# The first layer's first weights decoded from a later attention step on, and a pair's pooled values summed six steps later

## The chip, the core and the metric

The program runs on one core of one Trainium2 chip. The metric is the device time of one execution in microseconds (us), from launch to end. The kernel before took 979.33 us (median of three runs, 978.94 to 981.45). The core has five instruction streams that count here: PE (TensorE, matmuls, with its weight loads listed as PEld), DVE (VectorE), ACT (ScalarE), POOL (GpSimd) and SP (SyncE), which only issues DMAs. Each engine takes its list in order, and a semaphore holds it at an instruction whose inputs or buffers aren't ready.

## The reference

Three stages follow each other. First an attention with two parts, for 4 batches, 8 heads, 576 positions and 64 features a head: one on values averaged over groups of four positions, spread out again, and a local one in which a position sees the three neighbours on either side. Their sum, laid out as 2304 tokens of 512 features, goes through two layers of the same shape, the first with SiLU, the second with ELU.

```python
q_d, k_d, v_d = (z.reshape(B, H, S // 4, 4, D).mean(axis=3) for z in (q, k, v))
out_up = np.repeat(sm_attn(q_d, k_d, v_d), 4, axis=2)
mask = np.abs(pos[:, None] - pos[None, :]) < 4
attn = softmax(np.where(mask, q @ k.T / 8, -1e9))
x = (out_up + attn @ v).transpose(0, 2, 1, 3).reshape(B * S, H * D)
h = x @ w_in            # 2304x512 by 512x2048
x = (h * sigmoid(h)) @ w_out
h = x @ w_in2
out = np.where(h > 0, h, np.exp(np.minimum(h, 0)) - 1) @ w_out2
```

q, k, v and the weights arrive as they are drawn; the weights of both layers are 64-bit floats.

## The kernel before

**Attention.** Two heads are one pair, so there are 16 pairs, numbered 0 to 15, four a batch. `attention(i)` (L282) is a generator with 18 yields, so 19 steps: one call of `step()` (L681) advances one live pair to its next yield, so that several pairs are interleaved in the lists of all engines. Its parts, in order: transposition of q and k on PE (L297) with copies by ACT (L305, L307); the sums over four positions (L310, DVE); local scores (L319, PE, tile `psl`) with mask (L326) and maximum (L333) on DVE and the subtraction on POOL (L334); **the pooled values**, two additions of four rows of v into `vt` (L341) and one into `vd` (L342), all on POOL; the loads of the next pair (`load_pair`) and of this pair's windows of v (`load_windows`); the averaged scores (L363), their exponentials with an accumulated sum (L377, ACT) and the small L381; the local exponential (L383, ACT); row sums and reciprocals on DVE and the rescaling on POOL (L388, L393); then, after two yields without work, the transpositions of the probabilities (L405, L414, PE) with copies by ACT (L406, L415); the averaged output (L422, PE, which reads `vd`) with its copy (L425, ACT); and the local output (L434) with an addition on DVE (L442).

**Weights.** A weight is a tile of 128x512 values, which has to become two 32-bit parts, `wh` and `wl`, whose sum is the value. Weights 0 to 15 serve the first eight units of the first layer, w_in and w_out by turns. For each, SP loads 512 KB into one of three staging buffers `ws` (L138 or L143); ACT makes the magnitude `pw` (L157) and scales the exponent word (L159); DVE joins them (L168, L169, L175), after which SP is given the next load (L176, `load_next`); ACT casts `wh` (L185) and POOL subtracts to get `wl` (L187). `small_first()` (L655) advances such a chain by one of its steps, with at most three chains open.

**The head.** The order of the lists in the head comes out of one loop (L713) that runs until the four pairs of the first batch are through. It counts the attention steps in `n`, and from the thirteenth on adds `EARLY_PACE` a step to a credit; for each whole unit of it a weight chain goes one step on:

```python
            early += EARLY_PACE if n > 12 else 0
            while early >= 1:
                early -= 1
                if first["next"] < N_EARLY or len(first["live"]) > 1:
                    small_first()
```

Weights that are left after the loop are made in `tick`, called between the matmuls of the layers. SP's list is written in the same order: a load of a weight stands where the chain that frees its buffer has come to L176, a load of a pair where the pair before it has come to L343.

**The layers.** A unit is 128 of the 2048 middle features for one block of tokens (256 in the first blocks). `g1` (L488) makes its h with twelve matmuls (L501, tile `ph`) from the two parts of x (`xh` by ACT at L462, `xl` by DVE at L465) and of w_in; the activation and its two parts follow (L518 to L530); three units later `g2` (L534) makes twelve matmuls with w_out (L565). The pairs of the later batches are stepped in `tick`, by a deadline, between these matmuls; pair 4 is the first of them.

Of the kernel before, what the change touches and what calls it, by code (L numbers as in the profile page):

```python
# [9 lines left out]
F32 = mybir.dt.float32  # L10
# [5 lines left out]
ALU = mybir.AluOpType  # L16
# [6 lines left out]
def attention_moe_moe2_kernel(ctx, tc, q, k, v, wi1, wo1, wi2, wo2, out):  # L23
    nc = tc.nc
    B, H, S, D = q.shape
    NT, DM = out.shape
    DFF = wi1.shape[1]
    P = 128
    FAC = 4
    SD = S // FAC  # L30
    HS = SD // 2
    NPAIR = H // 2
# [18 lines left out]
    STEPS = 19  # L51
    TICKS = 8
    DECODE_PACE = 1.5
    EARLY_PACE = 1.1
    N_EARLY = 13
    WARM, FILL = 9, (8, 4, 4, 4)
    GROUP = 3
# [26 lines left out]
    att = attn_pools.enter_context(tc.tile_pool(name="att", bufs=2))  # L84
# [109 lines left out]
    loaded = {}  # L194
# [5 lines left out]
    def borrow(i, name):  # L200
        at, n = {"qk": (S, 2 * S), "qkD": (3 * S, 2 * SD), "vd": (3 * S + 2 * SD, 2 * SD)}[name]
        return x32[:, pairs[i][1], at:at + n][:, :2 * 2 * D if name == "vd" else n]
# [53 lines left out]
    def warm(n):  # L256
        pz = ps_h.tile([P, 512], F32, tag="h", name="pz")
        for _ in range(n):
            nc.tensor.matmul(pz, wz[0][:, :P], wz[0][:, :512], start=True, stop=True)
# [19 lines left out]
    def ring(name, n):  # L279
        return att.tile([P, NW * WIN], F32, tag="ring", name=name, bufs=5)[:, :n]  # L280

    def attention(i):  # L282
# [11 lines left out]
        for parts in ([(0, c) for c in range(NTB - 1)], [(1, c) for c in range(NTB - 1)], [(0, NTB - 1), (1, NTB - 1)]):  # L294
# [4 lines left out]
            for which in range(2):  # L299
                n = TB * sum(w == which for w, _ in parts)  # L300
# [31 lines left out]
        mx = att.tile([P, NW, 1], F32, tag="mx", name="mx", bufs=4)  # L332
        nc.vector.tensor_reduce(mx, E3, axis=AX.X, op=ALU.max)  # L333
        nc.gpsimd.tensor_tensor(E3, E3, mx.to_broadcast([P, NW, WIN]), ALU.subtract)  # L334

        vt = ring("vt", 2 * 2 * 2 * D).rearrange("p (n r d) -> p n r d", n=4, r=2)
        vd = borrow(i, "vd") if i < NPAIR else att.tile([P, 4 * D], F32, tag="vd", name="vd", bufs=2)
        vd = vd.rearrange("p (n d) -> p n d", n=4)
        for j, vn in enumerate(loaded.pop((i, 2))):
            vn = vn.rearrange("p (a r d) -> p a r d", a=2, r=FAC)  # L340
            nc.gpsimd.tensor_tensor(vt[:HS, 2 * j:2 * j + 2], vn[:HS, :, 0:2, :], vn[:HS, :, 2:4, :], ALU.add)  # L341
        nc.gpsimd.tensor_tensor(vd[:HS], vt[:HS, :, 0, :], vt[:HS, :, 1, :], ALU.add)  # L342
        if NPAIR - 1 <= i < len(pairs) - 1:  # L343
            load_pair(i + 1)
        if i >= 2:
# [45 lines left out]
        for x, heads in EDs:  # L391
            n = heads.stop - heads.start
# [2 lines left out]
            )  # L395
        yield
        yield

        aT = ring("aT", NW // 2 * P).rearrange("p (s w) -> p s w", w=P)
        if i < NPAIR:  # L400
# [26 lines left out]
        for t in range(2):  # L427
            ps = bank("pso")
            for w in range(t * NW // 2, (t + 1) * NW // 2):
                n = a0[w + 1] - a0[w]  # L430
# [164 lines left out]
    with tc.manual_schedule():  # L595
# [79 lines left out]
        def start_pair():  # L675
            i = state["next"]
            if i < state["limit"]:
                state["live"].append([pairs[i], attention(i), 0])
                state["next"] += 1
# [21 lines left out]
        def pending(b):  # L701
            return state["next"] < len(pairs) and pairs[state["next"]][0] <= b or any(x[0][0] <= b for x in state["live"])
# [6 lines left out]
        n = 0  # L709
        first_x = split_x(0, 0, 0)  # L710
        done = 0
        early = 0.0
        while pending(0):  # L713
            step()

            while done < NPAIR and state["next"] > done and pairs[done] not in [p for p, _, _ in state["live"]]:
                next(first_x)
                done += 1
            n += 1
            if n <= 16:  # L720
                warm(1)
            early += EARLY_PACE if n > 12 else 0
            while early >= 1:
                early -= 1
                if first["next"] < N_EARLY or len(first["live"]) > 1:
                    small_first()
# [48 lines left out]
        for i in range(len(units) + LAG):  # L775
            if i < len(units):
                layer, ps, n, f = units[i]
# [33 lines left out]
            if i >= LAG:  # L811
# [3 lines left out]
                layer, ps, n, f = u  # L815
# [32 lines left out]
```

## Time and profile before

| | |
|---|---|
| median of three runs | 979.33 us (978.94 to 981.45) |
| the profiled execution, its own time | 978.92 us |
| its span, first to last instruction | 977.1 us |
| mean granted clock of PE | 0.973 |
| busy, share of the span | PE 96%, PEld 82%, DVE 52%, ACT 45%, POOL 36% |
| busy from 0 to 100 us | PE 72.3, DVE 68.2, ACT 60.8, POOL 55.9 us |
| busy from 100 to 300 us | PE 193.5, DVE 91.2, ACT 101.5, POOL 94.0 us |
| busy from 300 us to the end | PE 669.6, DVE 352.4, ACT 277.2, POOL 203.2 us |
| device memory | 62.39 MB read, 14.16 MB written |

The profiled execution lies 0.4 us under the median, within the three runs. The busy shares of the whole span are averages over the head, in which the attention of the first batch and the first weights are made, and the layers, which hold nearly all the matmuls; the rows by stretch keep them apart. A wait in the trace is the idle time of an engine ahead of an instruction, with what released it in brackets. The granted clock is 1.00 for 2.4 GHz and 0.50 for 1.2 GHz.

### The profile page before, as it was taken

The page shows a single profiled execution, that of the slowest core. Times are in us where ns is not written, and L with a number is a line of the kernel's source. Part 1 is how long each engine was busy: PE and PEld are TensorE (multiplying, and loading weights), DVE is VectorE, ACT ScalarE, POOL GpSimd, SP SyncE. Part 2 cuts the span into 40 slices and gives each one's busy share as a digit, 9 for nine tenths or more (in the row PEclk, how much of TensorE's full clock was granted, in tenths as well). Part 3 has the DMA queues.
Part 4 walks back from the last instruction along what each step waited for, and adds up shares of the span by engine and source line. Part 5 has one row for each costly group of instructions (what it writes and reads, how often), then busy time and mean ns, then how long its engine had stood idle before and what let it go on. Part 6 is the DMA issues. An engine that isn't in the chain of part 4 may idle for free.

```text
span 977.1 us, 16442 instructions
## 1 busy us (share of the span) xinstructions
PE 935.5 (96%) x6493; PEld 805.0 (82%) x6493; DVE 511.7 (52%) x841; ACT 439.4 (45%) x995; POOL 353.1 (36%) x363
## 2 busy tenths in 40 slices
PE   6588999999999999999999999999999999999998
PEld 3357888999989999988888887888888888888886
DVE  4786554454446776654554367656544544434332
ACT  3686454545536666543434345434333433232221
POOL 3675544455452245322223433222233522222221
PEclk9677999999999999999999999999999999999999
DMA  9775342332212650422221103221101011112021
GB/s 181 168 191 159 85 113 70 85 93 71 79 37 87 177 169 35 126 78 87 65 66 64 44 1 87 87 87 44 65 0 44 1 65 65 44 44 86 1 87 44
DMA packets 93484, 77.60 MB, mean 79 GB/s; under 512 B 61664, under 2 KB 82144, under 8 KB 92384
## 3 DMA queue, kind: packets, MB, share of 16 engines
q1 hardware_dynamic: 91008, 75.97, 27.1%
q8 instruction: 51, 0.84, 0.4%
q10 hardware_dynamic: 2400, 0.59, 0.3%
q14 instruction: 25, 0.20, 0.1%
HBM read 62.39 MB, written 14.16 MB: 78 GB/s over the span
## 4 chain that ended last, share of the span: by engine, by line
PE 62%; ACT 1%; DVE 1%; issue 1%; DMA 0%; SPq 0%; DVEq 0%; ACTq 0%
PE ph L501 31%; PE y L567 19%; PE y L565 12%; DMA ws<-in_moe_w_out_dram 0%; DVE part L588 0%; DVE t L523 0%; ACT t L524 0%; ACT xh L462 0%; DVE xl L465 0%; ACT ws L159 0%; ACT gh L528 0%; ACT wf L157 0%; ACT wh L185 0%; DVE wf L169 0%; DVE wf L168 0%
## 5 line engine op out<-in xcount | busy, mean ns | idle before, releaser
L530 POOL TENSOR_TENSOR gl<-t,gh 128x256 fp32r<-128x256 f32 (+1 forms) x192 | 204.6, 1066 | 519.3 <-ACT gh L528 464.9
L501 PE MATMUL ph<-xh,wh 128*128 128x256 f32 (+1 forms) x768 | 252.2, 341 | 3.8 <-ACT xh L462 2.2
L501 PE MATMUL ph<-xl,wh 128*128 128x256 f32 (+1 forms) x768 | 250.9, 339 | 1.8 <-DVE xl L465 1.6
L501 PE MATMUL ph<-xh,wl 128*128 128x256 f32 (+1 forms) x768 | 179.8, 339 | 0.0
L501 PEld LDWEIGHTS ph<-xh,wh 128*128 128x128 f32 x768 | 146.5, 191 | 21.6 <-ACT xh L462 2.8
L501 PEld LDWEIGHTS ph<-xl,wh 128*128 128x128 f32 x768 | 146.5, 191 | 19.1 <-DVE xl L465 3.2
L528 ACT CAST gh<-t 128x256 fp32r<-128x256 f32 (+1 forms) x192 | 98.7, 514 | 120.2 <-DVE t L520 67.7
L565 PE MATMUL y<-gh,wh 128*128 128x256 f32 (+1 forms) x448 | 146.1, 326 | 1.3 <-DVE yo L578 1.3
L501 PEld LDWEIGHTS ph<-xh,wl 128*128 128x128 f32 x768 | 129.1, 191 | 15.3 <-issue 0.2
L565 PE MATMUL y<-gl,wh 128*128 128x256 f32 (+1 forms) x448 | 141.2, 315 | 0.0
L565 PE MATMUL y<-gh,wl 128*128 128x256 f32 (+1 forms) x448 | 141.1, 315 | 0.0
L520 DVE SCALAR_TENSOR_TENSOR t<-t,ph 128x256 f32<-128x256 f32 (+1 forms) x112 | 55.3, 494 | 160.3 <-ACT t L518 159.4
L524 ACT ACTIVATE t<-t 128x512 f32<-128x512 f32 (+1 forms) x80 | 47.1, 589 | 195.6 <-DVE t L523 195.6
L523 DVE TENSOR_SCALAR t<-ph 128x512 f32<-128x512 f32 (+1 forms) x80 | 51.0, 637 | 122.3 <-PE ph L501 121.9
L567 PE MATMUL y<-wh,gh 128*128 128x512 f32 x288 | 112.2, 390 | 0.0
L567 PE MATMUL y<-wh,gl 128*128 128x512 f32 x288 | 112.2, 390 | 0.0
L567 PE MATMUL y<-wl,gh 128*128 128x512 f32 x288 | 112.0, 389 | 0.0
L518 ACT ACTIVATE t<-ph 128x256 f32<-128x256 f32 (+1 forms) x112 | 49.6, 443 | 116.4 <-PE ph L501 113.8
L565 PEld LDWEIGHTS y<-gh,wh 128*128 128x128 f32 x448 | 86.3, 193 | 9.7 <-issue 2.1
L465 DVE TENSOR_TENSOR xl<-x,xh 128x256 fp32r<-128x256 f32 (+1 forms) x96 | 69.4, 740 | 45.1 <-ACT xh L462 43.4
L565 PEld LDWEIGHTS y<-gl,wh 128*128 128x128 f32 x448 | 86.4, 193 | 5.0
L565 PEld LDWEIGHTS y<-gh,wl 128*128 128x128 f32 x448 | 86.2, 192 | 5.0
(90 smaller groups left out, 1211.4 us busy)
## 6 DMA issues: line engine op xcount, KB each, us to landing
ws<-in_moe_w_in_dram SPq DMA_DIRECT2D x32, 512.0 KB
ws<-in_moe_w_out_dram SPq DMA_DIRECT2D x32, 512.0 KB
rows<-in_v_dram SPq DMA_DIRECT2D x36, 144.0 KB
yp<-yo SPq DMA_DIRECT2D x10, 512.0 KB
part<-yp SPq DMA_DIRECT2D x10, 512.0 KB
out_dram<-part SPq DMA_DIRECT2D x18, 256.0 KB
yp<-yo SPq DMA_DIRECT2D x4, 1024.0 KB
part<-yp SPq DMA_DIRECT2D x4, 1024.0 KB
```

Of the source, the lines that this page charges most:

```text
L465: nc.vector.tensor_tensor(lo[c - 1], src[:, c - 1, :], hi[c - 1].bitcast(F32), ALU.subtract)
L501: nc.tensor.matmul(ph[:, :nb], a[:, c, :], b[c], start=m == 0, stop=m == 3 * KC - 1)
L518: nc.scalar.activation(t, h, AF.Tanh, scale=0.5)
L520: nc.vector.scalar_tensor_tensor(t, t, 1.0, h, op0=ALU.add, op1=ALU.mult)
L523: nc.vector.tensor_scalar_min(t, h, 0.0)
L524: nc.scalar.activation(t, t, AF.Exp)
L528: nc.scalar.copy(gh, t)
L530: nc.gpsimd.tensor_tensor(gl, t, gh.bitcast(F32), ALU.subtract)
L565: nc.tensor.matmul(y[d // share][:, h:h + nb], wm[:, sl], gm, start=first and d % share == 0, stop=last, skip_group_check=True)
L567: nc.tensor.matmul(y[d], gm[:, sl], wm, start=first, stop=last)
```

## The change

Three edits, all to the order in which instructions are written. The weight chains of the head are begun from the twenty-fifth attention step on instead of the thirteenth. The credit for each step is 1.2 instead of 1.1. And the three additions of the pooled values, for all sixteen pairs before at one place ahead of the loads, become a function that is called at the old place for the pairs of the later batches, and six yields later, behind the rescaling and two empty yields, for the four pairs of the first batch. What is computed stays the same.

```diff
--- before.py
+++ after.py
@@ -51,7 +51,7 @@
     STEPS = 19
     TICKS = 8
     DECODE_PACE = 1.5
-    EARLY_PACE = 1.1
+    EARLY_PACE = 1.2
     N_EARLY = 13
     WARM, FILL = 9, (8, 4, 4, 4)
     GROUP = 3
@@ -332,14 +332,19 @@
         mx = att.tile([P, NW, 1], F32, tag="mx", name="mx", bufs=4)
         nc.vector.tensor_reduce(mx, E3, axis=AX.X, op=ALU.max)
         nc.gpsimd.tensor_tensor(E3, E3, mx.to_broadcast([P, NW, WIN]), ALU.subtract)
-
-        vt = ring("vt", 2 * 2 * 2 * D).rearrange("p (n r d) -> p n r d", n=4, r=2)
-        vd = borrow(i, "vd") if i < NPAIR else att.tile([P, 4 * D], F32, tag="vd", name="vd", bufs=2)
-        vd = vd.rearrange("p (n d) -> p n d", n=4)
-        for j, vn in enumerate(loaded.pop((i, 2))):
-            vn = vn.rearrange("p (a r d) -> p a r d", a=2, r=FAC)
-            nc.gpsimd.tensor_tensor(vt[:HS, 2 * j:2 * j + 2], vn[:HS, :, 0:2, :], vn[:HS, :, 2:4, :], ALU.add)
-        nc.gpsimd.tensor_tensor(vd[:HS], vt[:HS, :, 0, :], vt[:HS, :, 1, :], ALU.add)
+        def pooled_values():
+
+            vt = ring("vt", 2 * 2 * 2 * D).rearrange("p (n r d) -> p n r d", n=4, r=2)
+            vd = borrow(i, "vd") if i < NPAIR else att.tile([P, 4 * D], F32, tag="vd", name="vd", bufs=2)
+            vd = vd.rearrange("p (n d) -> p n d", n=4)
+            for j, vn in enumerate(loaded.pop((i, 2))):
+                vn = vn.rearrange("p (a r d) -> p a r d", a=2, r=FAC)
+                nc.gpsimd.tensor_tensor(vt[:HS, 2 * j:2 * j + 2], vn[:HS, :, 0:2, :], vn[:HS, :, 2:4, :], ALU.add)
+            nc.gpsimd.tensor_tensor(vd[:HS], vt[:HS, :, 0, :], vt[:HS, :, 1, :], ALU.add)
+            return vd
+
+        if i >= NPAIR:
+            vd = pooled_values()
         if NPAIR - 1 <= i < len(pairs) - 1:
             load_pair(i + 1)
         if i >= 2:
@@ -395,6 +400,9 @@
             )
         yield
         yield
+        if i < NPAIR:
+
+            vd = pooled_values()
 
         aT = ring("aT", NW // 2 * P).rearrange("p (s w) -> p s w", w=P)
         if i < NPAIR:
@@ -719,7 +727,7 @@
             n += 1
             if n <= 16:
                 warm(1)
-            early += EARLY_PACE if n > 12 else 0
+            early += EARLY_PACE if n > 24 else 0
             while early >= 1:
                 early -= 1
                 if first["next"] < N_EARLY or len(first["live"]) > 1:
```

The first place is ACT in the head, around the magnitudes of the first weights. ws_137, ws_148 and ws_159 are the staging buffers of weights 0, 1 and 2; E_247 is the local attention of pair 0, rows1_113 and rows1_114 the averaged probabilities of pair 1; pst is a result of a transposition. Before:

```order
L381 ACTIVATE sm_301<-sm_301 72x4
L157 ACTIVATE pw_369<-ws_137 128x512
L159 ACTIVATE ws_137<-ws_137 128x512
L307 COPY x32_98<-pst_377 128x480
L157 ACTIVATE pw_386<-ws_148 128x512
L159 ACTIVATE ws_148<-ws_148 128x512
L383 ACTIVATE E_247<-E_247 128x640
L305 ACTIVATE x32_98<-pst_417 128x96
L307 COPY x32_98<-pst_417 128x96
L185 CAST wh0_422<-wf_392 128x512
L157 ACTIVATE pw_432<-ws_159 128x512
L159 ACTIVATE ws_159<-ws_159 128x512
```

and in the changed kernel, from the same position of the list:

```order
L386 ACTIVATE sm_297<-sm_297 72x4
L307 COPY x32_98<-pst_368 128x480
L388 ACTIVATE E_247<-E_247 128x640
L305 ACTIVATE x32_98<-pst_395 128x96
L307 COPY x32_98<-pst_395 128x96
L382 ACTIVATE rows1_113,sm_383<-psd_387,nm_393 72x144 x2
L305 ACTIVATE x32_98<-pst_436 128x480
L382 ACTIVATE rows1_114,sm_383<-psd_388,nm_409 72x144 x2
L386 ACTIVATE sm_383<-sm_383 72x4
L157 ACTIVATE pw_447<-ws_137 128x512
L159 ACTIVATE ws_137<-ws_137 128x512
L307 COPY x32_98<-pst_450 128x480
```

Weight 0's L157 stood behind L381 of pair 0 and ahead of its local exponential, with weights 1 and 2 within the next ten rows; now the exponentials of pairs 0 and 1 stand ahead of weight 0.

The second place is SP, around the loads of pair 4. Before, with weights 6, 7 and 8 in ws_566, ws_614 and ws_646:

```order
L138 DMA ws_566<-in_moe_w_in_dram 128x4x256
L143 DMA ws_614<-in_moe_w_out_dram 128x1024
L138 DMA ws_646<-in_moe_w_in_dram 128x4x256
L238 DMA rows0_655<-in_q_dram 96x6x64 x2
L238 DMA rows1_658<-in_k_dram 96x6x64 x2
L215 DMA rows2_661<-in_v_dram 72x512 x2
L249 DMA rows0_131<-in_v_dram 64x9x64
```

and in the changed kernel, with weights 4, 5 and 6 in ws_524, ws_577 and ws_648:

```order
L138 DMA ws_524<-in_moe_w_in_dram 128x4x256
L143 DMA ws_577<-in_moe_w_out_dram 128x1024
L238 DMA rows0_621<-in_q_dram 96x6x64 x2
L238 DMA rows1_624<-in_k_dram 96x6x64 x2
L215 DMA rows2_627<-in_v_dram 72x512 x2
L249 DMA rows0_131<-in_v_dram 64x9x64
L253 DMA rows0_131<-in_v_dram 64x64
L249 DMA rows0_131<-in_v_dram 64x9x64
L253 DMA rows0_131<-in_v_dram 64x64
L138 DMA ws_648<-in_moe_w_in_dram 128x4x256
```

The loads of pair 4 and the windows of pair 3 (the rows into rows0_131) stood behind the load of weight 8; now they stand behind weight 5 and ahead of weight 6.

The third place is PE, the last rows up to the first local score of pair 4 (tile psl). ph is a unit's h, y the second product, pst the transpositions of pair 4. Before:

```order
L501 MATMUL ph_1104<-xl_944,wh0_754 128x256
L501 MATMUL ph_1104<-xh_942,wh0_754 128x256
L501 MATMUL ph_1104<-xl_989,wh0_754 128x256
L297 MATMUL pst_1118<-ident_96,rows0_655 128x96
L297 MATMUL pst_1118<-ident_96,rows1_658 128x96
L501 MATMUL ph_1104<-xh_987,wh0_754 128x256
L501 MATMUL ph_1104<-xl_994,wh0_754 128x256
L501 MATMUL ph_1104<-xh_785,wl0_755 128x256
L501 MATMUL ph_1104<-xh_876,wl0_755 128x256
L501 MATMUL ph_1104<-xh_942,wl0_755 128x256
L501 MATMUL ph_1104<-xh_987,wl0_755 128x256
L319 MATMUL psl_1138<-qk_1082 64x64
```

and in the changed kernel:

```order
L573 MATMUL y1_1107<-gl_1005,wh1_565 128x256
L573 MATMUL y1_1107<-gh_1004,wl1_566 128x256
L297 MATMUL pst_1134<-ident_96,rows1_624 128x96 x5
L573 MATMUL y1_1107<-gh_1004,wh1_565 128x256
L573 MATMUL y1_1107<-gl_1005,wh1_565 128x256
L573 MATMUL y1_1107<-gh_1004,wl1_566 128x256
L297 MATMUL pst_1147<-ident_96,rows0_621 128x96
L297 MATMUL pst_1147<-ident_96,rows1_624 128x96
L509 MATMUL ph_1157<-xh_756,wh0_889 128x256
L509 MATMUL ph_1157<-xl_857,wh0_889 128x256
L509 MATMUL ph_1157<-xh_855,wh0_889 128x256
L319 MATMUL psl_1163<-qk_1118 64x64
```

Before, 48 matmuls of the first block, all of L501, stand ahead of that score; in the changed kernel there are 63, with the first twelve of the second product and three of a fifth unit.

## Rows read from the trace of the kernel before

**Rows 1.** The page: its first line and the busy tenths of PE in 40 slices.

```profile
span 977.1 us, 16442 instructions
...
PE   6588999999999999999999999999999999999998
```

**Rows 2.** Table of stretches: span; busy us of PE, PEld, DVE, ACT, POOL; clock; DMA; GB/s.

```profile
16.30:31.15 14.85, 4.35 (x60) 2.79 (x58) 7.92 (x15) 4.25 (x9) 7.79 (x12) 0.65 1.10 194
31.15:50.00 18.85, 12.23 (x97) 7.45 (x99) 14.46 (x26) 13.46 (x39) 11.40 (x14) 0.68 0.60 153
50.00:72.11 22.11, 18.36 (x235) 13.04 (x231) 17.89 (x34) 20.34 (x49) 16.66 (x18) 0.74 0.77 183
```

**Rows 3.** Timeline of PE: first matmul of the first layer; scores of pair 4.

```profile
72.11 0.39 PE L501 MATMUL ph<-xh,wh 128*128 128x256 f32 x1
...
85.82 1.35 PE L319 MATMUL psl<-qk 64*64 64x64 f32 x40 [2.15 <-ACT qk L307]
```

**Rows 4.** Waits of ACT, 16 to 88 us: total us, times, longest.

```profile
ACT pw L157 <- DMA ws<-in_moe_w_in_dram: 6.0, 2, 3.0
ACT pw L157 <- DMA ws<-in_moe_w_out_dram: 4.9, 2, 4.6
```

**Rows 5.** Timeline of ACT: start, us, instruction, idle before it and its releaser.

```profile
19.29 0.62 ACT L157 ACTIVATE pw<-ws 128x512 f32<-128x512 f32 x1 [3.02 <-DMA ws<-in_moe_w_in_dram]
...
25.53 0.62 ACT L157 ACTIVATE pw<-ws 128x512 f32<-128x512 f32 x1 [4.60 <-DMA ws<-in_moe_w_out_dram]
...
31.15 0.63 ACT L157 ACTIVATE pw<-ws 128x512 f32<-128x512 f32 x1 [3.02 <-DMA ws<-in_moe_w_in_dram]
31.72 0.65 ACT L159 ACTIVATE ws<-ws 128x512 uint32<-128x512 uint32 x1
...
35.74 0.64 ACT L157 ACTIVATE pw<-ws 128x512 f32<-128x512 f32 x1 [0.29 <-DMA ws<-in_moe_w_out_dram]
...
51.76 0.62 ACT L157 ACTIVATE pw<-ws 128x512 f32<-128x512 f32 x1
```

**Rows 6.** Groups of ACT by line and form, 20 to 100 us: busy us, mean ns.

```profile
L377 ACT ACTIVATE rows<-psd,nm 72x144 f32<-72x144 f32 x12 | 4.4, 375 | 0.0
...
L415 ACT COPY aD<-psD 72x288 f32<-72x288 f32 x8 | 3.0, 394 | 0.6 <-PE psD L414 0.6
...
L425 ACT COPY x<-psu 128x576 f32<-128x576 f32 x4 | 2.5, 632 | 0.0
...
L377 ACT ACTIVATION_READ_ACCUMULATOR rows<-psd,nm 72x1 f32 x12 | 2.4, 201 | 0.0
...
L406 ACT COPY aT<-psE 128x256 f32<-128x256 f32 x4 | 1.5, 378 | 0.0
...
L381 ACT ACTIVATE sm<-sm 72x4 f32<-72x4 f32 x4 | 0.8, 205 | 0.1
```

**Rows 7.** DMA issues, 0 to 110 us: count and KB of each.

```profile
ws<-in_moe_w_in_dram SPq DMA_DIRECT2D x11, 512.0 KB
...
vw<-in_v_dram SPq DMA_DIRECT2D x8, 144.0 KB
```

**Rows 8.** Chain that ended last, in order of time: start, us, what.

```profile
354.72 1.44 PE y L565 x12
```

**Rows 9.** Group of POOL, 20 to 100 us: first step of the pooled sums.

```profile
L341 POOL TENSOR_TENSOR vt<-rows 72x256 f32<-72x256 f32 x10 | 7.1, 725 | 9.6 <-DMA rows<-in_v_dram 9.4 <-POOL E L334 0.2
```

**Rows 10.** Line L465 (60 to 125 us): ns min/median/max, first start; and POOL's timeline.

```profile
L465 DVE TENSOR_TENSOR xl<-x,xh x8: 408/426/1732, 66.4 to 110.8; 128x256 fp32r<-128x256 f32 x8
...
65.34 2.51 POOL L187 TENSOR_TENSOR wl<-wf,wh 128x512 fp32r<-128x512 f32 x2
```

**Rows 11.** Table of stretches, around the scores of pair 4 (columns as rows 2).

```profile
85.80:91.00 5.20, 5.18 (x59) 4.47 (x60) 4.94 (x9) 2.03 (x8) 3.54 (x4) 0.50 0.54 148
...
79.00:85.80 6.80, 3.99 (x33) 3.42 (x32) 3.92 (x8) 4.83 (x12) 3.15 (x4) 0.98 0.63 205
...
91.00:93.00 2.00, 1.57 (x12) 1.31 (x10) 0.00 (x0) 0.34 (x2) 1.92 (x4) 0.67 1.07 173
```

## The prediction

> **What bounds the kernel now.** The page comes first: over a span of 977.1 us PE is busy in at least nine tenths of every slice from the fifth to the one before last [rows 1]. What stands behind the first 90 us or so is therefore a queue of matmuls that nothing thins out much, and a change to the head counts by how much earlier PE gets through the same list. Next the table of stretches [rows 2]: from 16.3 to 31.15 us no engine is half busy but POOL and DVE, ACT works 4.25 of 14.85 us, and the DMA engines are full at 194 GB/s; from 31.15 to 50 us ACT has 13.46 of 18.85 us, and from 50 us to the first matmul of the first layer at 72.11 us [rows 3] it has 20.34 of 22.11 us. So the head is bound first by transfers that ACT waits for and then by ACT. The waits of ACT say which transfers: the first decode step of a weight (L157) waited 6.0 and 4.9 us for staging buffers [rows 4], and the timeline gives dates: weight 0 at 19.29 us after 3.02 us of waiting, weight 1 at 25.53 after 4.60, weight 2 at 31.15 after 3.02, weight 3 at 35.74 after 0.29 [rows 5]. ACT takes its list in order, so while it stands at one of these every later copy, exponential and transposition result of the attention stands behind it, though its data are there. Weights 0 to 15 here are the first block's, in order.
>
> **What the change does to ACT.** In the new order ACT does the attention instructions first, and only then turns to weight 0. I compared, at each weight's L157, what stands ahead of it in the two lists. The casts of weights are the same in number, and ahead by 3 to 4 us of attention work in the new list, from weight 0 to weight 8. The dates of weights 0 to 3 cannot move, since the transfers up to weight 3 are issued in the same order and the DMA engines are full; so at 19.29 and 25.53 us the waits turn into attention work, weight 2 is still awaited until about 31.15 and weight 3 until about 35.7 us, but ACT arrives there with more done.
>
> What counts is how much of that lead is left when ACT becomes the bound. At weight 6 (51.76 us before [rows 5]) the new list is ahead by four exponentials with their accumulator reads, one L381, two L415, one L425 and one L406 of 256 columns. By their means that is 4 x (375 + 201) + 205 + 2 x 394 + 632 + 378 = 4.3 us [rows 6]. Spans of neighbours on ACT overlap by about 0.06 us (31.15 plus 0.63 against the next start at 31.72 [rows 5]); with 13 instructions that takes off 0.8, which leaves **3.5 us**.
>
> Weight 6 must not come later for this to hold. On SP its load now stands behind the rows and windows of pair 4 and pair 3, which used to follow weight 8. After weight 3 has landed the queue holds two sets of windows (each 2 x 144 KB, their small rests left out), weights 4 and 5, six loads of 144 KB for pair 4 and weight 6: 576 + 1024 + 864 + 512 = 2976 KB [rows 7], 3.05 MB. At 194 GB/s it lands 15.7 us after 35.74, at 51.4 us; at 183 GB/s, the rate from 50 to 72 us, at 52.4 [rows 2]. So it is just as late as before, neither term nor loss: the lead stays 3.5 us, and its bounds are 0 (a slower queue) and 3.5.
>
> **The rest of the decode.** From weight 6 until the scores of pair 4 (L319) at 85.82 us, which PE enters after waiting 2.15 us for ACT's copies [rows 3], ACT has the same list in both kernels, in another order: all weights but the last cast stand ahead of those copies before and after. One weight fewer is cast ahead of the first tanh (11 against 12), so the first block begins with one more to do; since ACT binds through both, this moves work but adds none. Taken at nothing, bounded by one weight's share of that stretch, (85.82 - 72.11) / 4 casts = 3.4 us, as a loss.
>
> **PE at that place.** Pair 4 begins one unit later in the new order: 63 matmuls of the first block stand ahead of its scores instead of 48, so 15 fall into time in which PE waited for ACT. At full clock 12 take 1.44 us [rows 8], so 15 take **1.8 us**; at half clock 3.6. Bounds 0 and 3.6; I take 1.8.
>
> **The pooled sums.** Two L341 and one L342 per pair at 725 ns each [rows 9], 2.2 us, move six steps back on POOL, behind the rescaling of the same pair, for four pairs. POOL was not bound by work here but by their data: L341 waited 9.4 us for rows of v [rows 9], so leaving early costs nothing and lets the next score subtraction pass. They are only read by L422, after four copies of ACT. For the last pair nothing comes behind to cover them: 0 if ACT is later, 2.2 us if POOL is. I take **1.0 us** as a loss. The step pace (1.1 to 1.2) is contained in the lists compared. The 76 steps of the second batch start one unit later under the same deadline; I cost that at nothing because PE is nine tenths busy from there on [rows 1], and if that cover fails it is a wait such as the 2.15 us above.
>
> **Rule against the change.** The difference x - xh (L465, DVE, both inputs in SBUF) has a median of 426 ns but took 1732 ns once, at 66.4 us, while two subtractions on POOL ran from 65.34 to 67.85 [rows 10]. The sums now run later, nearer to the four L465 that open the first block. The Trainium skill (SBUF — State Buffer, Who interferes with whom) says that such an instruction and a GpSimd one that reads SBUF exclude each other, the later one blocking in full. The long row agrees. By that row each L465 that meets POOL costs up to 1.3 us, four of them 5.2; by the median nothing. I take nothing, because one of eight was hit.
>
> **Sum.** -3.5 - 1.8 + 1.0 = -4.3 us. The profiled execution took 978.92 us (span 977.1 and 1.8 around it) against a median of 979.33, so 974.6 on its scale, **975.0 us** on the median's.
>
> **Rivals.**
> *The transfers take the lead back.* At 153 GB/s, the lowest rate of the head's stretches [rows 2], 3.05 MB need 19.9 us and weight 6 comes at 55.7, 3.9 us late; that eats 3.5 and adds 0.4. The late sums then lie under the wait: 978.92 - 1.8 + 0.4 = 977.5, **977.9** as a median. For it: small packets of the row loads ahead of a weight. Against: 153 stands in a stretch where DMA was only 0.60 busy.
> *The port.* All four L465 meet POOL: 975.0 + 5.2 = **980.2**. It decides if they start inside a POOL instruction.
> *Slower: the decode chain binds the first block.* If the first matmul does not come earlier than 72.1 us (the lead gone at weight 6), five casts instead of four stand ahead of pair 4's scores: 85.82 + 3.4, and the 15 matmuls only fill a wait that this creates: 979.33 + 3.4 = **982.7**. Against: ACT's list is no longer in total, and at 72 us its lead is not all spent.
> *The clock.* PE was busy 3.99 of 6.80 us before 85.8, and then ran at half clock (granted 0.50, 1.2 GHz) to 91 and for a part of the next 2 us [rows 11]: 5.2 + 1.3 = 6.5 us, so 3.3 us lost. The 15 matmuls fill part of that idle time. If the half clock does not come, **971.7**. The Trainium skill (TensorE: Matmul & The Clock Gate, What's actually happening) says that the throttled state is the default and that activity releases it; the rows agree, with 0.50 after the idle stretch.
> *The change does not do what it says:* excluded, as the rows of the order have moved.
>
> **How the numbers follow.** A difference below 0.3% (2.9 us) cannot be told from none here; faster means under 976.4, slower over 982.3. Forecast 0.60, of which 0.52 below 976.4 (the lead and the 15 matmuls vary by 1 to 2 us); clock 0.07; transfers 0.14; port 0.07; decode chain 0.12. Faster 0.59, same 0.29, slower 0.12. The forecast alone spans 973 to 977.5; with the clock at one end and the port at the other the range is 971.5 to 980.2, which leaves out the decode chain and little else.
>
> **What would show it** (by the line numbers of before; the edit moves them by up to 8). Right: L157 no longer waits for weights 0 and 1 (7.6 us gone from ACT's waits), but still for weight 2 near 31 and weight 3 near 35.7; weight 6's L157 near 52 us; first L501 matmul near 68 to 70 us; pair 4's scores near 82 to 83, with 63 matmuls behind. Wrong: weight 6 after 54 us, L465 rows over 1 us, or the scores of pair 4 at 85 or later; or a head that is 4 us shorter and gives it back after 100 us.

## The result and the profile after

The changed kernel took **966.79 us** (median of 4 runs, 965.19 to 971.23) against 980.39 us (4 runs, 978.94 to 982.84): a ratio of 0.9893, 95% interval 0.9858 to 0.9927. The forecast was 975.0 us and its range began at 971.5. Two later series, each beside its own runs of the kernel before, gave 970.66 us (0.9926, 0.9900 to 0.9953) and 969.03 us (0.9903, 0.9869 to 0.9936). The three ratios have a mean of 0.9907, some 9 us of 978.5; the forecast was 4.3. So the direction held, and the forecast gave under half of the size. The 13.6 us of the first four runs are at the lucky end of the three series. The execution that was profiled took 971.23 us, the slowest of its four runs.

The page of the changed kernel, its first line and the tenths of PE, beside [rows 1]:

```profile
span 969.4 us, 16444 instructions
...
PE   8497999999999999999999999999999999999998
```

The first four slices, of 24 us each, read 8, 4, 9, 7 instead of 6, 5, 8, 8; from the fifth on PE is as full as before. The table of stretches, the same three as in [rows 2] (span; busy us of PE, PEld, DVE, ACT, POOL; clock; DMA; GB/s):

```profile
16.30:31.15 14.85, 7.28 (x124) 4.97 (x123) 11.32 (x23) 9.64 (x28) 9.17 (x13) 0.90 1.06 217
31.15:50.00 18.85, 12.45 (x96) 8.30 (x96) 14.22 (x27) 13.33 (x39) 13.65 (x16) 0.59 0.96 225
50.00:72.11 22.11, 21.75 (x187) 16.67 (x184) 15.75 (x31) 15.92 (x35) 13.12 (x14) 0.50 0.40 126
```

ACT did 9.64 us of work in the first stretch instead of 4.25, the DMA engines moved 225 GB/s in the second instead of 153, and in the third ACT had 15.92 us to do instead of 20.34. But PE went through that third stretch wholly at half clock, 0.50 instead of 0.74. The timeline of ACT, answering [rows 5], with weights 0, 1, 2, 3 and 6 and a copy of transposed probabilities (L414, L406 before):

```profile
20.39 0.63 ACT L157 ACTIVATE pw<-ws 128x512 f32<-128x512 f32 x1
...
24.58 0.63 ACT L157 ACTIVATE pw<-ws 128x512 f32<-128x512 f32 x1 [2.14 <-DMA ws<-in_moe_w_out_dram]
...
29.84 0.63 ACT L157 ACTIVATE pw<-ws 128x512 f32<-128x512 f32 x1 [2.64 <-DMA ws<-in_moe_w_in_dram]
...
35.45 0.63 ACT L157 ACTIVATE pw<-ws 128x512 f32<-128x512 f32 x1 [1.65 <-DMA ws<-in_moe_w_out_dram]
...
47.57 0.63 ACT L157 ACTIVATE pw<-ws 128x512 f32<-128x512 f32 x1 [0.26 <-DMA ws<-in_moe_w_in_dram]
...
50.89 0.48 ACT L414 COPY aT<-psE 128x384 f32<-128x384 f32 x1 [2.09 <-POOL x L343]
```

Its waits at L157 from 16 to 88 us, answering [rows 4]:

```profile
ACT pw L157 <- DMA ws<-in_moe_w_out_dram: 3.8, 2, 2.1
...
ACT pw L157 <- DMA ws<-in_moe_w_in_dram: 2.9, 2, 2.6
```

The first fell from 6.0 to 2.9, the second from 4.9 to 3.8 us. Weight 0 is no longer waited for at all; weights 1, 2 and 3 are, until 24.58, 29.84 and 35.45 us. Weight 6 is taken at 47.57, 4.2 us before the 51.76 of [rows 5]. The timeline of PE, answering [rows 3]:

```profile
66.66 0.58 PE L509 MATMUL ph<-xh,wh 128*128 128x256 f32 x1
...
82.91 1.35 PE L319 MATMUL psl<-qk 64*64 64x64 f32 x40 [0.44 <-ACT qk L307]
```

The first layer begins 5.45 us earlier, and the scores of pair 4 come 2.91 us earlier with 63 matmuls behind them.

Where the time went from there is read from the start of the same matmul of the layers in each trace (they come in one sequence in all kernels). The table gives it in us against the first profile of the kernel before; the four columns are matmuls number 1, 85, 361 and 1881, which that profile started at 72.1, 96.2, 163.6 and 398.7 us.

| profile | 1st | 85th | 361st | 1881st |
|---|---|---|---|---|
| kernel before, again | +3.1 | +3.0 | +1.5 | -0.2 |
| the change, first | -5.5 | -4.0 | -6.0 | -7.8 |
| the change, second | -5.0 | -5.7 | -6.4 | -6.9 |
| the change, third | -10.5 | -9.9 | -12.1 | -14.3 |
| decoding later only | -6.5 | -6.2 | -8.4 | -11.3 |
| the change, vt out of the ring | -11.5 | -11.0 | -13.2 | -15.6 |

Two profiles of one kernel differ by 3 us at the 85th matmul (before) and by 6 us (the change). Within that, the gain is there at the 85th matmul; behind it come 1 to 5 us that hang in part on where half-clock stretches fall (the first profile of the kernel before has two behind 100 us, at 153 and at 327 us; the second of the change, which gains least there, has two as well, at 148 and at 346 us).

### The profile page after: what moved, and what is told of

Same layout as the page of the kernel before. It is cut to its first block, busy times and chain, and to the rows that moved or that the text cites. A ratio compares the mean times of both kernels' runs of the same rounds, so it can differ in the third digit from the quotient of the medians.

```text
span 969.4 us, 16444 instructions
## 1 busy us (share of the span) xinstructions
PE 934.5 (96%) x6493; PEld 805.4 (83%) x6493; DVE 511.6 (53%) x841; ACT 438.7 (45%) x995; POOL 353.1 (36%) x363
## 4 chain that ended last, share of the span: by engine, by line
PE 62%; DVE 1%; ACT 1%; issue 0%; DMA 0%; SPq 0%; DVEq 0%; ACTq 0%
PE ph L509 31%; PE y L575 19%; PE y L573 12%; DMA ws<-in_moe_w_out_dram 0%; DVE part L596 0%; DVE xl L473 0%; DVE t L531 0%; ACT t L532 0%; ACT xh L470 0%; DVE wf L175 0%; DVE wf L168 0%; ACT gh L536 0%; DVE wf L169 0%; ACT ws L159 0%; ACT wf L157 0%
## 5 line engine op out<-in xcount | busy, mean ns | idle before, releaser
L509 PEld LDWEIGHTS ph<-xh,wl 128*128 128x128 f32 x768 | 129.0, 191 | 15.6 <-issue 0.6
L473 DVE TENSOR_TENSOR xl<-x,xh 128x256 fp32r<-128x256 f32 (+1 forms) x96 | 68.3, 729 | 45.3 <-ACT xh L470 44.7
```

The source lines that it names most:

```text
L473: nc.vector.tensor_tensor(lo[c - 1], src[:, c - 1, :], hi[c - 1].bitcast(F32), ALU.subtract)
L509: nc.tensor.matmul(ph[:, :nb], a[:, c, :], b[c], start=m == 0, stop=m == 3 * KC - 1)
```

## The experiments

Every kernel was timed beside the kernel before on the same chip, whose medians in those series were 978.3 to 979.2 us. Ratios have their 95% interval in brackets.

### The change and the kernel before, once more

> The changed kernel once more, for a second profile. Its first profiled execution took 971.23 us at a mean granted clock of 0.975, its other runs 965.2 to 968.0 at 0.980 to 0.984. Theory A (the order alone decides; the clock plays no part in the gain): first matmul of the first layer again at 66 to 67 us in the profile, time near 967. Theory B (the execution that was profiled first lost 4 to 6 us to half clock between 28 and 72 us, which other executions don't): where the mean clock is 0.98 or above, the first matmul of the first layer comes at 61 to 64 us and the time is 965 to 966.

> The kernel before once more, for a second profile. Theory A (half clock behind 100 us is chance, and the changed kernel's first profile was merely without it): the half clock at 153 and 327 us, 3.4 us each, comes at other places or not at all, first matmul of the first layer at 72 us plus or minus 0.7, scores of pair 4 at 85.8 plus or minus 1. Theory B (it belongs to the order): half clock at 153 and 327 us again.

> The changed kernel a third time. Theory A (its gain is what the ten runs so far give together, 8 to 9 us): 969 to 971 us beside 978 to 979. Theory B (the first four runs, 966.79, are its true time): 966 to 968 us.

The change: 970.66 and 969.03 us, as told above. The kernel before: 978.88 us, 1.0001 [0.9979 to 1.0024]. Its second profile had no half clock from 88 to 400 us, so that at 153 and 327 us is chance; but it began the first layer at 75.17 us and had pair 4's scores at 88.58, outside what theory A gave, and weight 6 at 48.9 instead of 51.8. A single profile places the end of the head only within some 3 us. Of the change, the second profile had a mean clock of 0.970, its first layer at 67.11 us and 972.15 us in all, the third 0.984, 61.58 and 966.24: as theory B of the second run has it, a higher clock goes with a first layer some 5 us earlier; two profiles don't show which of the two is the cause. For the medians theory A of the third run holds, 969 to 971 us.

### The two parts alone

```diff
-    EARLY_PACE = 1.1
+    EARLY_PACE = 1.2
...
-            early += EARLY_PACE if n > 12 else 0
+            early += EARLY_PACE if n > 24 else 0
```

> The kernel before with weight chains begun from the twenty-fifth step and a credit of 1.2; the pooled values stay at their old place. Theory A (the gain is ACT no longer standing at weights 0 and 1): 12 us of the 13.6 are here, 966 to 969 us. Theory B (the sums hold POOL until rows of v land, so that pair 1's subtraction still comes at 23 us and what ACT was to do ahead of weight 0 isn't there): half or less, 972 to 977 us.

971.24 us, 0.9927 [0.9899 to 0.9955]: 7.1 us faster, between the theories and by the time nearer to B. But the whole change took 970.66 us in the same series, only 0.6 us less, so by the share of the gain it is nearer to A. What B named is there all the same. POOL of this kernel (timeline: start, us, instruction, idle before it and its releaser), the first sum and the first rescaling:

```profile
18.00 0.73 POOL L341 TENSOR_TENSOR vt<-rows 72x256 f32<-72x256 f32 x1 [5.12 <-DMA rows<-in_v_dram]
...
25.58 1.25 POOL L388 TENSOR_TENSOR E<-E,rl 128x640 f32<-128x640 f32 x1
```

and ACT, the first copy of transposed probabilities and then weight 1:

```profile
27.88 0.48 ACT L406 COPY aT<-psE 128x384 f32<-128x384 f32 x1 [3.80 <-PE psE L405]
28.25 0.64 ACT L157 ACTIVATE pw<-ws 128x512 f32<-128x512 f32 x1
```

POOL stands 5.12 us for pair 0's rows of v; pair 1's subtraction, pair 1's sums and only then pair 0's rescaling follow. PE's transposition waits for that, ACT's copy for PE, and weight 1, awaited until 24.58 us in the change, is taken at 28.25.

The other part, the diff of `pooled_values` without those two lines:

> The kernel before with the pooled values of the first four pairs six steps later; weight chains as before, from the thirteenth step at 1.1. Theory A (the gain is ACT's): ACT still stands at weights 0 and 1 until 19.3 and 25.5 us, so within 2 us of the kernel before, 978 to 981 us. Theory B (a share of the gain of its own, from POOL and from the 3.7 us that ACT waited at 47 us for a ring buffer): 3 to 6 us faster, 974 to 977 us.

982.67 us, 1.0041 [1.0015 to 1.0066]: 4 us slower, which neither theory had. POOL, the sums of pair 1 and behind them the subtraction of pair 3:

```profile
51.20 1.41 POOL L342 TENSOR_TENSOR vt<-rows 72x256 f32<-72x256 f32 x2 [5.10 <-issue]
...
53.38 1.26 POOL L334 TENSOR_TENSOR E<-E,mx 128x640 f32<-128x640 f32 x1
```

The sums wait 5.10 us for nothing that the profile shows, and the subtraction, at 49.89 us in the kernel before, comes at 53.38. vt shares five buffers (`ring`) with E, aT and aD; moved back, it may ask for one when more of them are taken. The row doesn't say so, and the next kernel tests it.

```diff
-        vt = ring("vt", 2 * 2 * 2 * D).rearrange("p (n r d) -> p n r d", n=4, r=2)
+        vt = gp.tile([P, NBM], F32R, tag="gl", name="vt", bufs=LAG + 1).bitcast(F32) if i < NPAIR else ring("vt", 2 * 2 * 2 * D)
+        vt = vt.rearrange("p (n r d) -> p n r d", n=4, r=2)
```

> Sums six steps later alone (982.67 us, 4 slower than before), and vt out of the ring. Theory A (the loss is POOL waiting 5.1 us at 46 us for a ring buffer, with pair 3's subtraction behind it, 53.4 instead of 49.9 us): the subtraction back at 50 us or earlier and the loss gone, 977 to 980 us. Theory B (the loss is the position of the sums in POOL's list, ahead of the next subtraction): still 980 to 983 us.

979.51 us, 1.0013 [0.9992 to 1.0033]. The same two places:

```profile
45.39 1.42 POOL L343 TENSOR_TENSOR vt<-rows 72x256 f32<-72x256 f32 x2
...
49.56 1.26 POOL L334 TENSOR_TENSOR E<-E,mx 128x640 f32<-128x640 f32 x1 [1.95 <-DVE mx L333]
```

The wait is gone, the subtraction is back at 49.56, and the time is no longer clear of the kernel before: theory A, though the intervals of the two kernels overlap. With the weights decoded as before, the sums' place is then worth nothing measurable.

### vt out of the ring, in the change

> The changed kernel, with the tile vt of the first four pairs in a buffer of the layers that lies idle in the head, instead of one of the five ring buffers that it shares with E, aT and aD. Theory A (the 5.0 us that POOL waited at 34 us ahead of pair 1's sums, and the 2.1 us that ACT waited for them at 49 us, come from the shared ring and lie on the path): both waits gone, first matmul of the first layer 2 to 4 us before 66.7, 2 to 4 us faster than the change. Theory B (PE at half clock sets the end of the head): within 1 us of the change.

> The change with vt out of the ring again. Theory A (the shared ring costs the changed kernel 3 to 4 us): 965 to 968 us, 2 to 5 us faster than change_third. Theory B (the difference of the first series was chance): within 1 us of change_third.

966.58 us, 0.9877 [0.9852 to 0.9902], and again 967.06 us, 0.9885 [0.9858 to 0.9912]. POOL, the sums of pair 1, in the change:

```profile
38.92 1.42 POOL L342 TENSOR_TENSOR vt<-rows 72x256 f32<-72x256 f32 x2 [5.04 <-issue]
```

and with vt out of the ring:

```profile
33.46 1.42 POOL L343 TENSOR_TENSOR vt<-rows 72x256 f32<-72x256 f32 x2
```

5.04 us of waiting are gone. Pair 0's rescaling, which decoding later alone had at 25.58 us, no longer stands behind the sums and comes in this kernel at

```profile
19.32 1.26 POOL L394 TENSOR_TENSOR E<-E,rl 128x640 f32<-128x640 f32 x1 [1.87 <-DVE sm L396]
```

In the first pair of profiles the first layer begins at 60.56 us instead of 66.66, but the third profile of the change had 61.58 with the shared ring, so most of that distance lies between executions of one kernel. Beside one another the last two series differ by 2.0 us, and their intervals overlap: theory A is likely, at the small end of what it gave. It beats the kernel before clearly, and has the lowest medians with the sums later.

### The pace, the warming matmuls, the start

> The changed kernel with the old credit of 1.1 a step. Theory A (start and sums carry the gain, the pace is idle): 966 to 969 us, like the change. Theory B (the lower pace leaves more weights for the first block, where ACT binds): 1 to 4 us slower than the change, 968 to 971 us.

972.92 us, 0.9935 [0.9914 to 0.9957]. In its profile the first layer began at 61.44 us, and at the 121st matmul 3.0 of the 10.7 us of lead were spent; the third profile of the change, with 10.5 us of lead, kept 9.9. Pair 4's transposition waited 3.29 us behind DVE's decoding and pair 5's rows came 3.12 us late, instead of 2.05 and 1.77 us there. That is what theory B names, and the time leans to it; the intervals do not part it from the change.

> The changed kernel without the four warming matmuls each (tile pz, 1.9 us at half clock) ahead of the transpositions of pairs 2 and 3; nothing of the result hangs on them. Theory A (from 46 to 72 us PE, at half clock and without a gap, is what the end of the head waits for): first matmul of the first layer at 63 to 65 us instead of 66.7, 2 to 4 us faster than the change. Theory B (ACT's list sets it, PE's full rows are filler): first matmul within 0.7 us of 66.7. Theory C (less activity keeps the clock low for longer): first matmul earlier, the time not.

```diff
-    WARM, FILL = 9, (8, 4, 4, 4)
+    WARM, FILL = 9, (8, 4, 0, 0)
```

969.45 us, 0.9913 [0.9889 to 0.9938], and the first matmul of the first layer on PE's timeline:

```profile
66.56 0.58 PE L509 MATMUL ph<-xh,wh 128*128 128x256 f32 x1
```

By the number theory B: 3.8 us of PE rows could leave and the first layer began where it had. Where pair 3's warming matmuls stood, PE now waits for POOL's rescaling:

```profile
55.26 0.90 PE L413 MATMUL psE<-ident,E 128*128 128x128 f32 x3 [2.20 <-POOL E L393]
```

So the warming matmuls were filler. That PE is not the bound isn't shown by it: from this row to the first layer PE is full at half clock in both kernels, and where it had the full clock there (third profile of the change) the first layer began at 61.58 us.

> The change with vt out of the ring, weight chains from the nineteenth step on instead of the twenty-fifth. Theory A (what counts is that ACT does the attention work that is ready before it stands at weights 0 and 1): between the change with vt out and the kernel before, ACT waits 2 to 4 us more at weights 0 and 1, 968 to 973 us. Theory B (any start gives the same, since transfers up to weight 3 set the dates): 965 to 968 us.

> The change with vt out of the ring, weight chains from the thirty-first step on. Theory A (the waits at weights 0 to 3 are used up by the twenty-fifth step, and each further weight comes later than its transfer): weight 6 at 49 us or later instead of 46.6, 1 to 5 us slower than the 966.58 of vt out, 968 to 972 us. Theory B (ACT's list is no longer in total whatever the start): 965 to 968 us.

The nineteenth step: 968.23 us, 0.9891 [0.9858 to 0.9924], and 4.00 us of waiting at weight 1 instead of 1.64. That is within theory A by 0.2 us, and the interval does not part it from the twenty-fifth step. The thirty-first: 981.06 us, 1.0027 [1.0002 to 1.0052], 14 us slower than the twenty-fifth and far beyond what theory A gave. Weight 6 comes at 48.3 us and the first layer at 63.50, so the head isn't the place. PE's timeline of that kernel, its only two waits that end between 82 and 100 us:

```profile
82.62 0.92 PE L297 MATMUL pst<-ident,rows 96*128 96x96 f32 x5 [4.83 <-DVE wf L175]
...
93.69 1.03 PE L297 MATMUL pst<-ident,rows 96*128 96x96 f32 x5 [4.43 <-DMA rows<-in_q_dram]
```

Too many weights are left for the first block. Pair 4's transposition waits 4.83 us behind DVE's decoding, weight 15 is begun at 81.45 us, and pair 5's rows, loaded from pair 4's steps, are 4.43 us late in turn; with the twenty-fifth step the same two waits are 2.04 and 2.60 us. The lead of 8.6 us at the first matmul is still 7.9 at the 85th and 1.4 at the 121st. Between these two lie the second wait and a stretch, from 93 to 100 us, in which PE was granted 0.51; how much of the loss is the clock's isn't separated.

### Pair 4's loads

```diff
-        if NPAIR - 1 <= i < len(pairs) - 1:
+        if NPAIR <= i < len(pairs) - 1:
             load_pair(i + 1)
...
             vd = pooled_values()
+        if i == NPAIR - 1:
+            load_pair(i + 1)
```

> The change with vt out of the ring, and pair 4's loads six steps later, so that on SP weights 6 to 10 stand ahead of them instead of behind. The prediction had weight 6 wait for these 864 KB. Theory A (weight 6's transfer sets the date at which ACT takes it): weight 6 3 to 4 us before 46.6 and 2 to 4 us faster, unless pair 4's rows are then late. Theory B (ACT comes to weight 6 when its list lets it, the transfer is in time either way): weight 6 within 0.7 us of 46.6, time within 1.5 us of 966.58, or slower where pair 4's transposition waits for its rows.

966.95 us, 0.9886 [0.9857 to 0.9915]. Weight 6 with the loads behind it:

```profile
45.63 0.63 ACT L157 ACTIVATE pw<-ws 128x512 f32<-128x512 f32 x1
```

and with them ahead, as in the change:

```profile
46.63 0.63 ACT L157 ACTIVATE pw<-ws 128x512 f32<-128x512 f32 x1 [0.35 <-DMA ws<-in_moe_w_in_dram]
```

1.0 us earlier, without a wait; theory B holds for the time, and its 0.7 us was a little narrow. The second profile of the kernel with the loads ahead has weight 6 at 48.49 after a wait of 2.02 us, so its transfer does bind there, by an amount that differs between executions, and the time doesn't follow.

### Rows of v ahead of weight 0

What remained was why the later sums gain 6 us when decoding is later too (972.65 against 966.58, vt out of the ring in both):

> Weight chains from the twenty-fifth step at 1.2, the sums at their old place, vt out of the ring. It asks what the sums' place is worth when the ring doesn't hold POOL. Theory A (the later place is worth something by itself: POOL isn't held by rows of v ahead of the next pair's subtraction): 970 to 972 us, as with the ring (971.24), against 966.58 for the change with vt out. Theory B (the place is worth nothing, only the ring costs): 966 to 968 us.

972.65 us, 0.9932 [0.9906 to 0.9959]: theory A. To take POOL's wait away in another way, the sums stay at their old place and the rows come earlier.

```diff
-        load_next()
         load_rows(0, 2)
+        load_next()
         load_windows(0)
```

> Decoding later alone (971.24 us), and pair 0's rows of v loaded ahead of weight 0 instead of behind it; sums at their old place. Theory A (the later sums gain because POOL doesn't stand until the rows of v land): POOL's first L341 waits 1 to 2 us less than 5.1, more if the rows land earlier still, weight 1 at 25 to 27 us instead of 28.2, 967 to 970 us. Theory B (the interaction has another cause): 970 to 973 us.

> The same with vt out of the ring (972.65 us without the earlier rows). Theory A: POOL's first sums at 16 to 17 us instead of 19.4, weight 1 at 25 to 27 us instead of 29.6, 967 to 970 us, near the 966.58 of the later sums. Theory B: 971 to 974 us.

972.36 us, 0.9930 [0.9901 to 0.9959], and 971.22 us, 0.9928 [0.9905 to 0.9952]: no gain, weight 1 at 29.0 and 28.7 us, by the numbers theory B. POOL of the second, the sums of pairs 0 and 1 and pair 0's rescaling:

```profile
16.05 1.55 POOL L342 TENSOR_TENSOR vt<-rows 72x256 f32<-72x256 f32 x2 [2.93 <-DMA rows<-in_v_dram]
...
23.84 1.47 POOL L342 TENSOR_TENSOR vt<-rows 72x256 f32<-72x256 f32 x2 [4.18 <-DMA rows<-in_v_dram]
...
26.11 1.25 POOL L389 TENSOR_TENSOR E<-E,rl 128x640 f32<-128x640 f32 x1
```

The wait had only moved: pair 0's sums start at 16.05 us, but pair 1's stand until 23.84 for their own rows, and pair 0's rescaling is behind them. So both pairs' rows went first:

```diff
-        load_next()
         load_rows(0, 2)
+        load_rows(1, 2)
+        load_next()
         load_windows(0)
         load_next()
-        load_rows(1, 2)
         load_windows(1)
```

> Decoding later with vt out of the ring, sums at their old place (972.65 us), rows of v of pairs 0 and 1 both loaded ahead of weight 0. Theory A (POOL held by rows of v is what the later sums remove): POOL waits under 3.5 us for rows of v instead of 7 to 8, pair 0's rescaling at 20 to 23 us instead of 27, its first transposed copy (aT) at 22 to 24 us instead of 29, weight 1 at 25 to 27 us, and 965 to 969 us like the later sums (966.58). Theory B (the sums' old place costs for another reason): the copy earlier, the time not, 970 to 974 us.

966.29 us, 0.9877 [0.9841 to 0.9913]. POOL, the same three places:

```profile
17.17 1.46 POOL L342 TENSOR_TENSOR vt<-rows 72x256 f32<-72x256 f32 x2 [3.95 <-DMA rows<-in_v_dram]
...
20.65 1.41 POOL L342 TENSOR_TENSOR vt<-rows 72x256 f32<-72x256 f32 x2
...
22.86 1.26 POOL L389 TENSOR_TENSOR E<-E,rl 128x640 f32<-128x640 f32 x1
```

and ACT, the first copy and weight 1:

```profile
24.76 0.48 ACT L407 COPY aT<-psE 128x384 f32<-128x384 f32 x1 [1.25 <-PE psE L406]
25.60 0.64 ACT L157 ACTIVATE pw<-ws 128x512 f32<-128x512 f32 x1 [0.37 <-DMA ws<-in_moe_w_out_dram]
```

The rescaling comes at 22.86 instead of 26.11 (26.97 with the rows in their old order), the copy at 24.76, weight 1 at 25.60, and the time is that of the later sums. Theory A for the rescaling, weight 1 and the time. Two numbers missed: the copy (22 to 24 expected), and POOL's waits for rows of v, which still sum to 7.2 us, 3.95 for pair 0 and 3.28 now for pair 2 at 30 us. That last wait isn't without a follower either: pair 1's rescaling stands behind it until 32.29, though DVE had its factors ready by 29.8 us. So it isn't POOL's waiting in sum that the two kernels at 966 us have less of, but the wait ahead of pair 0's rescaling. Putting both pairs' rows first also put the loads of weights 0 and 1 behind them (awaited 0.45 and 0.37 us); what that alone is worth was not tried.

## Why the prediction was wrong

**The step that failed is the pooled sums.** The prediction had it that "POOL was not bound by work here but by their data [...] so leaving early costs nothing and lets the next score subtraction pass", and entered +1.0 us, for the last pair only. The 9.4 us of [rows 9] were read as idle time of an engine off the path. They look like that in the kernel before: ACT stood at weights 1 and 2 until 31.15 us [rows 5], and what POOL held up wasn't asked for sooner (with the weights decoded as before and vt out of the ring, the later sums changed nothing: 1.0013). The same change takes ACT away from there, and then POOL's wait is what is late next: with decoding later alone pair 0's rescaling comes at 25.58, ACT's first copy waits 3.80 us and weight 1 comes at 28.25. Measured, the later sums are worth -6.1 us on top of the later decoding with vt out of the ring (972.65 to 966.58, in intervals that don't meet). The last experiment gets the same time from the rows' order, with the sums at their old place, though its interval just meets that of 972.65. So the cause is the wait for the rows of v ahead of pair 0's rescaling, and not the sums' place. In the change as it is, the ring seems to take part of it back: decoding alone has a ratio of 0.9927, the change 0.9907 as the mean of three, 2.0 us, and beside each other in one series the two differ by 0.6 us. Ratios of medians are uncertain here by about 0.3%, so in the change itself this term is not clear of nothing. The forecast lacked almost 5 us in all; how they divide between this term and the next one stays open.

**The lead of ACT and the 15 matmuls** were 3.5 and 1.8, 5.3 us together. Decoding later alone gave 7.1, in an interval of 4.4 to 9.9 us (0.9955 and 0.9899 of 978.5), and 5.9 with vt out of the ring (4.0 to 9.2): the terms stand within it, 1.8 us from the middle. Their working was half right. The 15 matmuls are there, 63 at the scores of pair 4. But weight 6 was said to be "just as late as before" because its transfer, in a queue that was to hold it from 35.74 us on, would land at 51.4 us. That date was wrong. On SP its load was issued, before:

```profile
42.49 0.39 SPq L138 DMA_DIRECT2D ws<-in_moe_w_in_dram  x1
```

and in the change:

```profile
43.49 0.53 SPq L138 DMA_DIRECT2D ws<-in_moe_w_in_dram  x1
```

In the change it was taken at 47.57, 4.1 us after its issue, with a wait for its transfer of 0.26; in the second and third profile at 48.68 and 47.31, after waits of 0.91 and 1.93. So the transfer did bind, but 3 to 4 us sooner than said. By the same 4.1 us the load before was in place at 46.6 us, an estimate from these rows; ACT came to it behind a copy that had itself waited 3.67 us for PE (ACT's timeline, before):

```profile
50.74 0.48 ACT L406 COPY aT<-psE 128x384 f32<-128x384 f32 x1 [3.67 <-PE psu L422]
```

The second profile of the kernel before had weight 6 at 48.9, so how much earlier the change takes it, 4.2 us or nearly nothing, differs with the profiles compared. The queue was as full as the prediction had it, but faster than the 194 and 183 GB/s that were used (the change, the columns of [rows 2]):

```profile
35.45:47.57 12.12, 7.56 (x74) 5.33 (x73) 9.27 (x18) 9.49 (x25) 8.51 (x11) 0.64 0.95 232
```

At 232 GB/s the 3.05 MB need 13.1 us, and from the 35.45 us of weight 3 they land at 48.6, an estimate from this row. And pair 4's loads ahead of it, which the whole estimate rested on, cost 1.0 to 2.9 us at weight 6 and nothing in the time (966.95 us without them, 966.58 and 967.06 with them).

**The rest of the decode** was taken at nothing, up to 3.4 us of loss. In the first profiles the lead is 5.45 us at the first matmul and 2.91 at the scores of pair 4, 2.5 less, of which the 15 matmuls that now stand ahead are 1.8; so 0.7 us were given back, well inside the bound. But this is the term that turns the curve: at the thirty-first step the rival "the decode chain binds the first block" is what happened. It had been given 982.7 us; 981.06 were measured there. That the numbers are so close is luck: the rival's condition was a first matmul no earlier than 72.1 us, and it came at 63.50.

**The rivals.** *The transfers take the lead back:* no; weights 1 to 3 are awaited, and weight 6 for 0.26 to 1.93 us in the three profiles, but at 47.3 to 48.7 us and not at 55.7. *The port:* no; the four subtractions xl (L473) took 415 to 615 ns in the change. The longest started at 58.07 while POOL was in pair 2's sums (57.68 to 59.28): 0.2 us above the median, not the 1.3 of [rows 10]. The Trainium skill (SBUF — State Buffer, Who interferes with whom) has the two exclude each other; this row shows a cost of that kind and no more than this size. *The clock:* the half clock at 85.8 came in the change as well (granted 0.66 from 82 to 87 us), so this rival's case did not arise; but the clock moved more in the head than the rival allowed (below).

**What the prediction named as its signs:** weight 0 without a wait, right; weight 1 without one, wrong, 2.14 us remain, and 4.2 us are gone from ACT's waits at L157 instead of 7.6; weights 2 and 3 still awaited, right; weight 6 near 52 us, missed (47.57); the first matmul at 68 to 70, missed (66.66); the scores of pair 4 at 82 to 83, right in the first profile (82.91), 83.51 and 79.40 in the others.

## What to carry to other kernels

A wait of an engine off the path is free only as long as the engine on the path is held elsewhere; when a change frees that one, go through every other wait in the same stretch and ask who stands behind it, two instructions further on as well. Where a step is moved, its buffers move with it: a tile from a shared ring, asked for later, waited 5 us for a buffer that it used to find free. And a start that pays when moved by twelve steps (13 to 25) lost everything with six more, with waits for the work put off from the head in the first block.

## What the runs showed of the hardware

Executions of one kernel differ, and the clock goes with it: 100 runs of the kernel before lie between 971.34 and 985.65 us, 18 of the change between 963.66 us at a mean granted clock of 0.985 and 974.88 us at 0.968. In the table of stretches, the change's first profile:

```profile
41.00:57.00 16.00, 12.12 (x96) 8.18 (x96) 12.37 (x26) 13.02 (x33) 14.01 (x17) 0.53 0.59 175
57.00:73.00 16.00, 15.64 (x133) 12.90 (x133) 11.38 (x22) 10.73 (x23) 8.78 (x9) 0.51 0.43 137
```

and its third:

```profile
41.00:57.00 16.00, 12.44 (x102) 8.41 (x102) 12.39 (x27) 12.83 (x34) 14.00 (x17) 0.57 0.70 179
57.00:73.00 16.00, 11.16 (x141) 9.63 (x138) 12.62 (x24) 12.37 (x27) 8.85 (x9) 1.00 0.48 144
```

From 57 to 73 us PE is granted 0.51 in the one and 1.00 in the other, and has 15.64 us of rows instead of 11.16 for much the same instructions; the third execution's first layer begins 5.1 us earlier. Before this stretch PE had been at 0.53 and 0.57, busy 12.12 and 12.44 of 16 us: its rows don't show why one went up and the other didn't. The Trainium skill (TensorE: Matmul & The Clock Gate, What's actually happening) says that the throttled state is the default and that activity releases it; here a PE that the profile has as busy for 15.64 of 16 us stayed at the lower clock, 1.2 GHz. The rows don't settle it. For the prediction it means that a change of the head of 4 us is of the size of what one profile can move by, and that the medians, not the profiles, carry its size.
